# Moving two output transposes from steps 8 and 9 to steps 12 and 13, and one eviction from VectorE to ScalarE

## The chip, the cores and the metric

The kernel runs on one core of a Trainium2 chip. Its engines are TensorE (PE in the profile; PEld is its weight load), VectorE (DVE), ScalarE (ACT), GpSimd (POOL) and SyncE (SP), whose queue issues nearly all DMAs here. The metric is the device time of one execution in microseconds, as the median of several runs.

## The reference

Two blocks follow one another. All data are 32-bit floats in the reference's terms; the weights arrive as 64-bit floats and are converted in the kernel.

```python
# attention: x is [8, 8, 512, 64], state is [8, 8, 32, 64]
a = softmax(scale * x @ state.T)          # per batch and head, 512 x 32
xread = a @ state                         # 512 x 64
a2 = softmax(scale * state @ x.T)         # 32 x 512
sread = a2 @ x                            # 32 x 64
attn = concatenate([xread, sread], axis=2)
# bridge: heads side by side, 8 * 544 tokens of 512
h = tokens @ w_in                         # 512 -> 2048
g = h * cos(h)
out = g @ w_out                           # 2048 -> 512
```

## The kernel before, in words

**Steps.** A batch is worked off in 16 steps, one for each 128 of the 2048 hidden columns (`NF` = 16, `NH` = 8, a half). Eight batches of 512 tokens make 128 steps; 16 more steps treat the 256 state rows of all batches together. The order of the work on every engine is written out by hand: the loop at the end of the function goes through the steps and emits the instructions in the order in which each engine's queue shall run them. "Step 8 of batch 3" below is the pass of that loop with `t.b` = 3 and `s` = 8.

**One step.** `hidden` (L471) lets PE compute h for the step into one of two PSUM buffers (`hps`, tile `h`, two buffers). Its weights `sw` are `w_in` already multiplied with the state (`products`, L319, copied out at L445), its moving operand is the attention `aT`. Then the cosine factor: `gate` (L567) on ScalarE rounds h, `gate2` (L570) on VectorE subtracts, `gate3` (L573) on ScalarE takes the sine, `gate4` (L580) on VectorE multiplies by h into a slot of `g_all`. With `gate4` the h buffer comes free, and as there are two, `hidden` of step s needs `gate4` of step s-2. Three steps later `output` lets PE multiply g with blocks of `w_out` (`product`, L624, in two PSUM banks, MAIN and SIDE, of two halves each).

**Seven products for eight.** The products with `w_out` are made for pairs of batches (0 and 1, 2 and 3, and so on) by a scheme that needs seven block products where the plain one needs eight, with sums of g blocks before (`minus`, L586, on VectorE and GpSimd) and of results behind. A pair's four phases are the two halves of the hidden columns of its two batches. Results that are needed again are kept in three `held` tiles: `keep_product` takes a finished product out of PSUM, one half with ScalarE (L635), the other with VectorE (L637); `plus` (L630) adds a product to a held one; `total` (L644) adds held ones. The first and the fifth product of each pair go through `keep_product`: the fifth at the end of step 10 of the pair's odd batch. For phases 0 to 2 of batches 2 to 7 `hidden` is replaced by a similar scheme with seven half-size products (`hidden_a`, `hidden_b`, L514, with sums at L544 to L546 and L559, L560).

**Stores.** `store` does not emit anything at once. It appends two entries to the list `later`, one for each half; so does `total`. Each step takes at most one entry out of `later`, between `gate3` and `gate4`. A store's entry is a transpose of 32 x 32 blocks on VectorE (L651) from the held tile into one of two `ot` buffers and four DMAs on SP's queue (L657).

In batches 3, 5 and 7 the last product of the pair before ends in step 7 (`p4`, which then queues the two stores of that pair's even batch, second half of its columns). So steps 8 and 9 take one entry each, and `later` is empty from then on until step 2 of the next batch.

**Attention beside it.** While batch b is worked off, `plan` spreads the attention of batch b+1 over the same steps: for batches 3 and 5 the tokens' transposes (L301) in steps 1 and 2, scores and maxima in steps 5 and 6 (L333, spread by L339 in step 6), the shift (L356), row maxima (L349) and exps (L360, L365) in steps 6 and 7, sums in step 8 (L333, L375, L376), the norm in step 9 (L386), the state's part on PE in steps 10 to 12 (`turn` L392, copied by L397; `reads` L409; `keep` L419). Behind the reads of step 12 SP issues the loads of x for a later batch (L292, L115). In step 11 of an odd batch VectorE forms the differences (`halves`, L493) that the next batch needs. Batch 7 has no next batch, and none of this.

**Tail.** In the 16 steps of the state rows two blocks of `w_out` are read again (L197 on SP, emitted in the first of them) into the place of x, and converted from step 5 and step 7 of that part on (L228 and what follows).

Of the kernel before, what the change touches and what calls it, by code (L numbers as in the profile page):

```python
# [13 lines left out]
ACTF = mybir.ActivationFunctionType  # L14
# [3 lines left out]
TWO_PI = 2.0 * math.pi  # L18
# [3 lines left out]
def kernel(  # L22
# [8 lines left out]
    nc = tc.nc  # L31

    B, H, S, D = x.shape
# [9 lines left out]
    scale = 1.0 / math.sqrt(D)  # L43
# [23 lines left out]
    NH = NF // 2  # L67
# [58 lines left out]
    def load_state(half, queues):  # L126
        b = slice(4 * half, 4 * half + 4)
        for k in range(NK):
# [11 lines left out]
    acc = [[ops.tile([P, S], F32, name=f"o{m}{ch}") for ch in range(2)]  # L140
           for m in range(2)]
# [311 lines left out]
    def part(b, name, *args):  # L453

        if b not in attn:
            attn[b] = Attention(b)
        getattr(attn[b], name)(*args)
        if (name, args) == ("reads", (1,)) and b + 1 < B:
            if b > 0:
                attn[b + 1] = Attention(b + 1)  # L460
                attn[b + 1].load_tokens()
            load_x(b + 1)
# [125 lines left out]
    MAIN, SIDE = 0, 1  # L588
# [33 lines left out]
    def product(bank, w, g, i):  # L622
        for ch in range(2):
            nc.tensor.matmul(out=acc[bank][ch],  # L624
                             lhsT=w[:, i, P * ch:P * ch + P], rhs=g.g,
                             start=(i == 0), stop=(i == NH - 1))
        return i == NH - 1

    def plus(out, bank, ch, b):
        nc.vector.scalar_tensor_tensor(out=out.t[:, ch], in0=acc[bank][ch],  # L630
                                       scalar=TWO_PI, in1=b.t[:, ch],
                                       op0=ALU.mult, op1=ALU.add)

    def keep_product(out, bank):
        nc.scalar.activation(out.t[:, 0], acc[bank][0], func=ACTF.Copy,  # L635
                             scale=TWO_PI)
        nc.vector.tensor_scalar(out.t[:, 1], acc[bank][1], TWO_PI, None,  # L637
                                op0=ALU.mult)

    later = []  # L640

    def total(out, a, b):
        for ch in range(2):
            later.append(lambda ch=ch: nc.vector.tensor_tensor(  # L644
                out.t[:, ch], a.t[:, ch], b.t[:, ch], op=ALU.add))

    def store(b, half, src):

        def go(ch):
            ot = osb.tile([P, S], F32, name="ot")  # L650
            nc.vector.transpose(out=ot.rearrange("p (j i) -> p j i", i=32),  # L651
                                in_=src.t[:, ch].rearrange(
                                    "p (j i) -> p j i", i=32))
            rows = out[b * T:b * T + S, :].rearrange("(j t) d -> t j d", t=32)
            for q in range(P // 32):
                c0 = HD * half + P * ch + 32 * q
                nc.sync.dma_start(  # L657
                    out=rows[:, :, c0:c0 + 32],
                    in_=ot[32 * q:32 * q + 32].rearrange(
                        "p (j i) -> p j i", i=32))  # L660
            src.done()
        later.extend([lambda: go(0), lambda: go(1)])
# [16 lines left out]
    def free(t):  # L679
        g_free.append(t.slot)  # L680
# [18 lines left out]
    def output(t):  # L699
        if t.pair is None:  # L700
            state_output(t)
            return
        pr, i = t.pair, t.i
        if t.phase < 3 and pr.before and i % 3 < 2:
            pr.before.more(1)
        if t.phase == 0:
            if product(MAIN, a11, t, i):
                pr.u = Held()
                keep_product(pr.u, MAIN)
        if t.phase == 1:  # L710

            bank = MAIN if pr.before else SIDE
            if product(bank, a12, t, i):
                o = Held()
                for ch in range(2):
                    plus(o, bank, ch, pr.u)
                store(2 * pr.n, 0, o)
        if t.phase == 2:
            if product(MAIN, s1, pr.b[0, i], i):
                pr.p5 = Held()  # L720
                keep_product(pr.p5, MAIN)
        if t.phase == 3:
            last = product(SIDE, s4, t, i)
            free(t)
            if last:
                o = Held()
                for ch in range(2):
                    plus(o, SIDE, ch, pr.p5)
            product(MAIN, s2, pr.b[0, i], i)
            free(pr.b[0, i])  # L730
            if last:
                for ch in range(2):
                    plus(pr.u, MAIN, ch, pr.u)
                total(o, o, pr.u)
                store(2 * pr.n + 1, 0, o)
# [12 lines left out]
    def state_output(t):  # L748
        if t.n_th < NF - N_LAST:
            for i in range(2):  # L750
                state_product(t, i)
            t.last_pair.more(2)
            free(t)
            return
        kept_back.append(t)
        if len(kept_back) == N_LAST:
            t.last_pair.more(2 * N_LAST)
            for i in range(2):
                for u in kept_back:
                    state_product(u, i)  # L760
                state_store(i)
# [36 lines left out]
    def warm(n, to):  # L798

        for _ in range(n):  # L800
            nc.tensor.matmul(out=to, lhsT=zeros[:, 0:P], rhs=zeros, start=True,
                             stop=True)
# [124 lines left out]
    for step, t in enumerate(all_tiles):  # L927
        s = step % NF
        if s == 0 and t.b < B:
            steps = plan(t.b)  # L930
        todo = [p[s] if t.b < B else [] for p in steps]

        def go(n):
            for p in todo[n]:
                part(*p)

        last, conv = conv_at.get(step - 1, -1), conv_at.get(step, -1)
        if step == B * NF + (0 if f64 else 8):
            fetch(N_LOADS + 2)
        if step == 4:  # L940
            warm(1, acc[MAIN][0])
        ahead = all_tiles[step + 1:step + 3]
        if seven(t):
            if t.f % 2 == 0:
                hidden_b(t)
                sums_b(t)
                if s == NF - 2 and seven(all_tiles[step + 2]):
                    halves(t.b + 1)
        elif step != 1:
            hidden(t)  # L950
        first = len(ahead) > 1 and seven(ahead[0]) and ahead[0].f % 2 == 0
        if first:
            if not seven(t):

                h = t.hp
                take_slot(t)
                nc.scalar.copy(t.g, h)
            hidden_a(*ahead)
        if step == 0:
            hidden(all_tiles[1])  # L960
            warm(3, acc[MAIN][0])
            gate(t)
            gate2(t)
            convert(3, "bcdf")
            convert(4, "1")
            go(0)
        else:
            go(0)
            if step == 5:
                states(1, acc[SIDE][1])  # L970
            if not (seven(t) and t.f % 2):
                gate(t)
            gate2(t)
            if step == 3:
                warm(4, acc[MAIN][0])
                part(0, "products", 1, SIDE)
            if first:
                sums_a(ahead[0])
            go(1)
            go(3)  # L980
            if step == 1:
                convert(4, "bcdf")
            elif last >= 0:
                convert(last, "bcdf")
            if conv >= 0 and not todo[1]:
                convert(conv, "1")
        gate3(t)
        if seven(t) and t.f % 2 == 0:
            gate(t.second)
        if step == 3:  # L990
            part(0, "products_kept", 1, SIDE)
        if later:
            later.pop(0)()
        for u, new in zip(all_tiles[step + 2:step + 4], (False, True)):
            if seven(u) and u.f % 2 == 0 and new_pair(u) == new:
                sw_sums(u)
        gate4(t)
        if conv >= 0 and todo[1] and step > 0:
            convert(conv, "1")
        if t.pair is not None:  # L1000
            sums(t)
        if step == 6:
            states_kept(1, acc[SIDE][1])
        go(2)
        if conv >= 0:
            convert(conv, "2")
        go(4)
        for u in all_tiles[step + 5:step + 6]:
            if seven(u) and new_pair(u):
                halves(u.b)  # L1010
        if step in block_at:
            blocks(*block_at[step])
        if t.pair is not None:
            sums2(t)
        while len(line) >= (LAG if step >= 2 * NH else LAG + 1):
            output(line.pop(0))
        line.append(t)
# [32 lines left out]
```

## Time and profile before

| what | value |
|---|---|
| median of 8 runs | 766.31 us (765.78 to 767.26) |
| the profiled execution's own time | 766.22 us |
| its span, first to last instruction | 764.4 us |
| granted TensorE clock, mean | 0.997 |
| PE busy | 751.8 us, 98% |
| VectorE busy | 520.4 us, 68% |
| ScalarE busy | 316.0 us, 41% |
| GpSimd busy | 249.5 us, 33% |
| L651 on VectorE | 32 instructions, 22.2 us, mean 692 ns |
| L637 on VectorE | 8 instructions, 5.4 us, mean 680 ns |
| L635 on ScalarE | 8 instructions, 4.7 us, mean 592 ns |
| output stores on SP (L657) | 128 DMAs of 64 KB, landing after 2.0 us in the median |

All times within the profile are microseconds from the start of the span. Durations of instructions that follow one another overlap a little, as an instruction may start before the one ahead has been drained; what an instruction adds to its engine's queue is read from start to start. Ends of matmuls are modelled, so PE's busy share says less than the distances between its starts. The chain of waits is followed back from the last instruction: a line's entry there is time that the end of the program hung on.

### The profile page before, as it was taken

To read this page: it belongs to the slowest core of one execution; us is meant where nothing else is said; L and a number is where in the kernel's file an instruction comes from. 1 tells how busy PE (TensorE), PEld (TensorE's weight loads), DVE (VectorE), ACT (ScalarE), POOL (GpSimd) and SP (SyncE) were. 2 spreads that over 40 slices of the span, in tenths; PEclk is the share of its full clock that TensorE was granted. 3 is DMA by queue.
4 is the path that set the end of the run, shared out by engine and by line. 5 is a ranking of instruction groups with operands and counts; after the bars stand their busy time and mean duration, and the time that the engine had idled before them with its cause. 6 is when DMAs were issued, how large, how long until landed. Compare 5 with 4: busy or idle time off the path is not lost.

```text
span 764.4 us, 8416 instructions
## 1 busy us (share of the span) xinstructions
PE 751.8 (98%) x2880; PEld 380.8 (50%) x2880; DVE 520.4 (68%) x862; ACT 316.0 (41%) x523; POOL 249.5 (33%) x258
## 2 busy tenths in 40 slices
PE   8998999999999999999999999999999999999997
PEld 4443443445555554445555553445555554455554
DVE  4778787836896788847886789747878676432431
ACT  3877944533254335333362336333443333212212
POOL 2344278777121210662221111751211206500200
PEclk9999999999999999999999999999999999999999
DMA  8595471060002510340105210420100115000021
GB/s 247 165 276 175 146 119 29 4 107 1 14 15 48 90 28 3 54 83 0 28 2 94 44 28 15 68 56 1 27 1 1 28 28 138 0 0 15 14 42 41
DMA packets 161962, 43.54 MB, mean 57 GB/s; under 512 B 153920, under 2 KB 153920, under 8 KB 161920
## 3 DMA queue, kind: packets, MB, share of 16 engines
q1 hardware_dynamic: 161024, 42.49, 25.6%
q10 hardware_dynamic: 768, 0.39, 0.2%
q8 instruction: 23, 0.38, 0.2%
q0 software_dynamic: 128, 0.13, 0.1%
q14 instruction: 19, 0.16, 0.1%
HBM read 34.08 MB, written 8.91 MB: 56 GB/s over the span
## 4 chain that ended last, share of the span: by engine, by line
PE 88%; DVE 7%; ACT 2%; issue 1%; DMA 1%; POOL 1%; SPq 0%; DVEq 0%; ACTq 0%; POOLq 0%
PE o L624 47%; PE h L514 14%; PE h L471 14%; PE at L319 4%; PE o L744 4%; PE at L409 2%; PE o L319 1%; DVE xT L339 1%; DVE q L570 1%; DVE g_all L580 1%; DVE i L333 1%; ACT q L567 1%; PE at L392 1%; DVE aT L356 1%; DMA x_b<-in_x_dram 1%
## 5 line engine op out<-in xcount | busy, mean ns | idle before, releaser
L624 PE MATMUL o<-g_all,w_out 128*128 128x512 f32 x512 | 236.4, 598 | 0.3 <-POOL w_out L242 0.3
L624 PE MATMUL o<-g_all,s 128*128 128x512 f32 x384 | 177.3, 598 | 0.0
L586 POOL TENSOR_TENSOR g_all<-g_all 128x512 f32<-128x512 f32 x80 | 112.8, 1434 | 120.3 <-DVE g_all L580 120.3
L624 PEld LDWEIGHTS o<-g_all,w_out 128*128 128x128 f32 x512 | 93.8, 190 | 112.7 <-issue 108.0
L573 ACT ACTIVATE q<-q,halfpi 128x512 f32<-128x512 f32 (+1 forms) x144 | 100.8, 700 | 97.3 <-DVE q L570 97.2
L624 PEld LDWEIGHTS o<-g_all,s 128*128 128x128 f32 x384 | 70.8, 190 | 88.1 <-issue 82.1
L570 DVE TENSOR_TENSOR q<-q,h 128x512 f32<-128x512 int32 (+1 forms) x69 | 42.8, 621 | 102.5 <-ACT q L567 102.5
L471 PE MATMUL h<-aT,sw 128*128 128x512 f32 x224 | 106.1, 597 | 4.8 <-DVE g_all L580 4.3
L567 ACT ACTIVATE q<-g_all 128x512 int32<-128x512 f32 x75 | 46.8, 624 | 141.8 <-DVE g_all L560 141.4
L567 ACT ACTIVATE q<-h 128x512 int32<-128x512 f32 (+1 forms) x69 | 37.6, 545 | 128.5 <-PE h L471 128.5
L570 DVE TENSOR_TENSOR q<-q,g_all 128x512 f32<-128x512 int32 x75 | 52.6, 702 | 35.5 <-ACT q L567 35.5
L471 PEld LDWEIGHTS h<-aT,sw 128*128 128x128 f32 x224 | 41.5, 190 | 60.2 <-issue 44.2
L509 POOL TENSOR_TENSOR swS<-sw 128x128 f32<-128x128 f32 x35 | 17.4, 496 | 148.6 <-PE h L514 107.3
L580 DVE TENSOR_TENSOR g_all<-g_all,q 128x512 f32<-128x512 f32 x75 | 53.9, 719 | 14.5 <-ACT q L573 14.4
L580 DVE TENSOR_TENSOR g_all<-h,q 128x512 f32<-128x512 f32 (+1 forms) x69 | 42.8, 620 | 23.5 <-ACT q L573 23.1
L242 POOL TENSOR_TENSOR w_out<-w_out,s 128x1024 int32<-128x1024 int32 x10 | 23.9, 2393 | 77.5 <-DVE w_out L237 71.3
L509 POOL TENSOR_TENSOR swS<-sw,swS 128x128 f32<-128x128 f32 x35 | 18.3, 523 | 87.3 <-PE h L514 86.8
L514 PEld LDWEIGHTS h<-aT,sw 128*128 128x128 f32 x144 | 27.4, 190 | 34.4 <-issue 28.0
L514 PE MATMUL h<-aS,sw 128*128 128x256 f32 x144 | 43.1, 381 | 0.1
L514 PE MATMUL h<-aS,swS 128*128 128x256 f32 x144 | 42.8, 379 | 0.0
L514 PE MATMUL h<-aT,sw 128*128 128x256 f32 x144 | 42.8, 379 | 0.0
L586 DVE TENSOR_TENSOR g_all<-g_all 128x512 f32<-128x512 f32 x48 | 33.5, 697 | 1.6
(107 smaller groups left out, 888.4 us busy)
## 6 DMA issues: line engine op xcount, KB each, us to landing
out_dram<-ot SPq DMA_DIRECT2D x132, 64.0 KB, 2.0
g_all<-in_moe_w_out_dram SPq DMA_DIRECT2D x8, 1024.0 KB, 5.0
g_all<-in_moe_w_in_dram SPq DMA_DIRECT2D x6, 1024.0 KB, 5.4
xT<-in_x_dram SPq DMA_DIRECT2D x96, 64.0 KB, 2.5
x_b<-in_x_dram SPq DMA_DIRECT2D x24, 256.0 KB, 4.6
x_b<-in_x_dram SPq DMA_DIRECT2D x16, 128.0 KB, 4.1
g_all<-in_moe_w_in_dram SPq DMA_DIRECT2D x4, 512.0 KB, 6.0
x_b<-in_moe_w_out_dram SPq DMA_DIRECT2D x1, 1024.0 KB, 5.7
```

The costliest lines, as they stand in the source:

```text
L242: nc.gpsimd.tensor_tensor(bits, bits, e, op=ALU.add)
L319: nc.tensor.matmul(out=(to or at)[j][Ns * k:Ns * k + Ns, 0:n], lhsT=w[D * j:D * j + D, self.b, Ns * k:Ns * k + Ns], rhs=r(slice(D * j, D * ...
L471: nc.tensor.matmul(out=t.hp, lhsT=t.lhs(i), rhs=t.rhs(i), start=(i == 0), stop=(i == t.kn - 1))
L509: engine.tensor_tensor(o, x1, x2, op=op)
L514: nc.tensor.matmul(out=out, lhsT=w, rhs=r, start=True, stop=True)
L567: nc.scalar.activation(t.q.bitcast(I32), t.hp, func=ACTF.Copy, bias=0.25)
L570: nc.vector.tensor_tensor(t.q, t.q.bitcast(I32), t.hp, op=ALU.subtract)
L573: nc.scalar.activation(t.q, t.q, func=ACTF.Sin, bias=halfpi, scale=-TWO_PI)
L580: nc.vector.tensor_tensor(t.g, t.hp, t.q, op=ALU.mult)
L586: engine.tensor_tensor(out, a, b, op=ALU.subtract)
L624: nc.tensor.matmul(out=acc[bank][ch], lhsT=w[:, i, P * ch:P * ch + P], rhs=g.g, start=(i == 0), stop=(i == NH - 1))
L744: nc.tensor.matmul(out=acc[MAIN][i], lhsT=t.g[:, P * i:P * i + P], rhs=w_out[:, :, t.f, :], start=(t.n_th == 0), stop=(t.n_th == NF - 1))
```

## The change

```diff
-    def keep_product(out, bank):
-        nc.scalar.activation(out.t[:, 0], acc[bank][0], func=ACTF.Copy,
-                             scale=TWO_PI)
+    def keep_product(out, bank, scalar=False):
+
+        for ch in range(2 if scalar else 1):
+            nc.scalar.activation(out.t[:, ch], acc[bank][ch], func=ACTF.Copy,
+                                 scale=TWO_PI)
+        if scalar:
+            return
         nc.vector.tensor_scalar(out.t[:, 1], acc[bank][1], TWO_PI, None,
                                 op0=ALU.mult)
...
         if t.phase == 2:
             if product(MAIN, s1, pr.b[0, i], i):
                 pr.p5 = Held()
-                keep_product(pr.p5, MAIN)
+                keep_product(pr.p5, MAIN, pr.n > 0)
...
-        if later:
+
+
+        full = t.b % 2 == 1 and 1 < t.b < B and NH - 1 <= s < NH + 4
+        if later and not full:
             later.pop(0)()
```

`full` is true in steps 7 to 11 of batches 3, 5 and 7. In these steps nothing is taken out of `later`; the two entries that wait there, which before were taken in steps 8 and 9, are taken in steps 12 and 13. With each entry its transpose (L651) and its four DMAs (L657) are emitted there. The held tile that they read is given back in step 13 instead of step 9; the tiles that `Held` hands out are the same as before in every place.

The fifth product of the pairs 1 to 3 (step 10 of batches 3, 5 and 7) is taken out of PSUM by two ScalarE instructions instead of one on ScalarE and one on VectorE. That of pair 0 stays as it was. Nothing else is added, removed or moved.

## The prediction

> **What bounds the kernel now.** The first part of the page and a table by stretch come first: which engine is full, and is it full everywhere? The stretches are 38 or 39 us around steps 7 to 12 of batches 3, 5 and 7.
>
> ```profile
> PE 751.8 (98%) x2880; PEld 380.8 (50%) x2880; DVE 520.4 (68%) x862; ACT 316.0 (41%) x523; POOL 249.5 (33%) x258
> 286.00:324.00 38.00, 37.02 (x148) 16.80 (x133) 34.01 (x54) 16.24 (x27) 12.56 (x9) 1.00 0.16 26
> 453.00:492.00 39.00, 38.03 (x151) 17.22 (x150) 34.40 (x55) 16.54 (x27) 13.28 (x9) 1.00 0.16 26
> 618.00:656.00 38.00, 38.00 (x110) 17.76 (x109) 23.12 (x36) 12.95 (x21) 15.03 (x10) 1.00 0.30 76
> ```
>
> Columns of the last three: length, then busy time of PE, PEld, DVE, ACT and POOL, then PE's clock. PE is the bound with 98%. What can be won without taking matmuls away is its idle time. Batches 3 and 5 show 0.98 and 0.97 us of it, beside a VectorE busy for 34 us; batch 7, which prepares no attention of a next batch, shows none. So the change can pay in two of its three batches only.
>
> Second, the chain of waits across batch 3's stretch: who carries the time while PE stands?
>
> ```profile
> 303.64 0.04 DVE i L376
> ...
> 303.92 0.65 DVE ot L651
> 304.57 0.59 DVE g_all L580
> ...
> 307.53 1.80 DVE aT L386
> 309.33 0.62 DVE ot L651
> 309.95 0.59 DVE g_all L580
> 310.54 0.04 issue
> 310.58 1.98 PE h L471 x4
> ```
>
> From 290.12 (L560) to 310.58 the chain lies on VectorE and, for the exps, on ScalarE; then it goes back to PE and stays there. The two L651 pieces are the transposes that steps 8 and 9 make for the stores: the change moves exactly these. L580 is the gate's last product; it frees the h buffer that `hidden` needs two steps on.
>
> Third, PE's own timeline there.
>
> ```profile
> 303.05 1.98 PE L624 MATMUL o<-g_all,s 128*128 128x512 f32 x4
> 305.20 1.99 PE L471 MATMUL h<-aT,sw 128*128 128x512 f32 x4 [0.18 <-DVE g_all L580]
> 307.02 1.04 PE L392 MATMUL at<-ident,xT 128*128 128x128 f32 x8
> 307.90 1.88 PE L624 MATMUL o<-g_all,s 128*128 128x512 f32 x4
> 310.58 1.98 PE L471 MATMUL h<-aT,sw 128*128 128x512 f32 x4 [0.80 <-DVE g_all L580]
> ```
>
> Ends are modelled, so I count from start to start. Four matmuls in an unbroken run take 1.72 us (296.78 to 298.50), and 1.82 behind the small ones of L319 (636.40 to 638.22 in batch 7). `hidden(10)` could start at 303.05 + 1.82 = 304.87 and starts at 305.20: 0.33 lost, and 0.10 more for the restart (1.82 to the next, not 1.72). `hidden(11)` could start at 307.90 + 1.72 = 309.62 and starts at 310.58: 0.96 lost, and 0.10 for the restart. PE loses 1.49 us per batch here; that is the most that any relief of VectorE can give.
>
> **The two transposes leave steps 8 and 9.** From L651's start to L580's start behind it: 303.92 to 304.50 is 0.58, 309.25 to 309.88 is 0.63; batch 5 has 0.58 and 0.62 (471.21 to 471.79, 476.54 to 477.16). Does L580 move forward by all of it? It also needs ScalarE's sine: in step 8 that ended at 303.48 (302.76 + 0.72), before the 303.92 at which L580 would now start; in step 9 it started at 307.64 behind VectorE's own L570, and moves with it. So L580 comes 0.58 earlier in step 8 and 1.21 earlier in step 9.
>
> One thing could eat the first 0.58. L386, the norm of step 9, took 1.80 us here against a median of 1.23 over the eight of the kernel, and GpSimd's two subtractions of step 8 ran from 305.23 to 308.24, into it. L386 ended 1.09 us after them, so it looks as if it had stood behind GpSimd. But that pair starts on L580 of step 8 (24.63 us waited for it, start 0.08 after its end): it moves 0.58 earlier with it, so I count the gain whole; with GpSimd fixed in time it would be 0.63 per batch. [...]
>
> On PE: `hidden(10)`'s buffer comes free for a start at 305.20 - 0.58 = 304.62, before the 304.87 at which PE is ready, so that wait goes. PE is then ready for `hidden(11)` at 304.87 + 1.72 + 0.88 (L392) + 1.72 = 309.19, and the buffer lets it start at 310.58 - 1.21 = 309.37. A wait of 0.18 is left, still on VectorE, so the gain is the chain's 1.21, not PE's 1.49. Batch 5 gives 1.20 in the same way. Behind it PE has work without a wait (buffer of `hidden(12)`: L580 ends at 313.33, PE comes at 317.06), so the gain is kept to the end. Batch 7: 0, no PE idle to remove.
>
> **The fifth product goes to ScalarE alone** (step 10 of batches 3, 5 and 7). These rows are batch 3's, from the timelines of VectorE and ScalarE.
>
> ```profile
> 313.36 0.80 DVE L586 TENSOR_TENSOR g_all<-g_all 128x512 f32<-128x512 f32 x1
> 314.09 0.68 DVE L637 TENSOR_SCALAR held<-o 128x512 f32<-128x512 f32 x1
> 314.69 0.67 DVE L570 TENSOR_TENSOR q<-q,h 128x512 f32<-128x512 int32 x1
> ...
> 312.98 0.60 ACT L635 ACTIVATE held<-o 128x512 f32<-128x512 f32 x1
> 313.46 0.60 ACT L567 ACTIVATE q<-h 128x512 int32<-128x512 f32 x1
> ```
>
> VectorE loses 0.60 (314.09 to 314.69), ScalarE gains 0.48 (312.98 to 313.46). What stands behind the new eviction on ScalarE is L567 of step 11, and L570 waits for that: it would end at 313.46 + 0.48 + 0.60 = 314.54 instead of 314.06, where L570 now starts at 314.69. So L570 of step 11 comes at best 0.1 earlier. Nobody on PE waits there: `hidden(13)` starts at 323.43 and its buffer was free at 316.84, 6.6 us before. Its new wait on PE ends before it begins (that product's matmuls end at 309.78), and the bank's second half is written again only from some 315.3 on. In batch 7 L567 of step 11 waited 0.87 us for PE behind L635, which holds the 0.48. I take 0; without the 6.6 us of cover it would be a loss of up to 0.48 per batch, and it can't gain, since PE is not idle there.
>
> **What the transposes meet in steps 12 and 13.** In step 12 one lies ahead of L580 (322.79), 0.6 us; in step 13 it falls into the 1.49 us that L580 waited for ScalarE (328.21). `hidden(14)` starts at 329.79 with its buffer free at 323.48, `hidden(15)` at 334.94 with 328.90: 6.3 and 6.0 us of cover for 0.6. The two `ot` buffers were last used in steps 3 and 4 and their stores land within 3.1 us. Cost 0.
>
> **The DMAs on SP's queue.** Each transpose takes four stores along. In batches 3 and 5 they go behind the twenty loads of x that step 12 issues (L292 from 313.66, L115 to 331.51), which can then not be held up by them; the stores' data is nobody's input. In batch 7 two reloads of weights (L197, issued at 639.56 and 640.13) now stand behind stores that leave only after step 13's transpose, near 655.9, with some 2 us of issue: about 18 us later. They land within 7.8 us, near 667, and ScalarE first reads them at 698.91: over 30 us of cover. Cost 0.
>
> **Sum.** 1.21 + 1.20 = 2.41 us from the profiled execution's 766.22 (span 764.4 and 1.8 around it) gives 763.81; the median of the runs, 766.31, lies 0.09 above that execution, so 763.9.
>
> **Rivals.** (a) *Half*: GpSimd's subtractions do not move with L580, and L386 still ends where it did; only the step 9 transposes count: 766.3 - 1.25 = 765.1. For it: the 1.80; against: the 0.08 us between L580's end and GpSimd's start. (b) *Nothing*: another wait of PE takes the place, most likely on ScalarE's L573 of steps 8 and 9: 766.3. Against: that sine was ready 0.44 us before the new start. (c) *All of PE's idle time*: shorter instructions on VectorE without the 0.18 left: 766.3 - 2 x 1.49 = 763.3. (d) *Slower*: batch 7's two reloads, put behind the moved stores, come late for L228 at 698.91, and with them the products that need that weight; PE stands for as long. It decides only when they land more than 30 us later than I work out, that is 50 us later than now. 4 us beyond that, about one step's PE work in batch 7, would leave 766.3 - 2.4 + 4 = 767.9. The queue order speaks for it, the margin against it. The edit itself does what it says: in each of the three batches exactly two transposes wait in steps 8 to 11, and steps 12 and 13 have nothing else to take.
>
> **Chances.** Forecast 0.79, (a) 0.08, (b) 0.06, (c) 0.03, (d) 0.04. A measurement of this kernel tells about 0.2%, 1.5 us, from no change. The forecast and (c) are beyond that: faster 0.82. (a) and (b) lie within: 0.14. Slower: 0.04. The range goes from (c), 763.2, to (a), 765.1; (b), (d) and a little of the edges are left out.
>
> **What would show it.** In the changed profile: no L651 between L376 and L580 in step 8, nor behind L386 in step 9; `hidden(10)` without its wait, `hidden(11)` with about 0.2 left; GpSimd's step 8 pair still 0.1 behind L580 and L386 still near 1.8; PE idle in the two stretches about 0.6 to 0.8 less in the table's modelled busy time; L635 eleven times, L637 five; L197 near 657; batch 7 without PE idle. L386 longer by 0.6 means (a); a PE wait on ScalarE in steps 8 to 11 means (b); a PE stop near 700 means (d).

## The result, and the profile after

The changed kernel takes 763.36 us in the median (762.58 to 764.44, 10 runs), the kernel before 766.06 (28 runs of the same session). The ratio is 0.9965, interval 0.9957 to 0.9973: 2.7 us less, from 2.1 to 3.3. The profiled execution of the changed kernel took 763.10 us with a span of 761.3.

Behind the fifth product's eviction the changed kernel's lines are shifted: the transpose for the store is L655 (was L651), the eviction on ScalarE L637 (was L635) and that on VectorE L641 (was L637). Everything up to the eviction has the lines that it had.

First the page's sum of busy time and the table by stretch, as before: length, then PE, PEld, VectorE, ScalarE, GpSimd, and PE's clock. The first two stretches hold steps 7 to 12 of batches 3 and 5, the third those of batch 7.

```profile
PE 750.1 (99%) x2880; PEld 380.2 (50%) x2880; DVE 519.2 (68%) x859; ACT 317.4 (42%) x526; POOL 249.7 (33%) x258
286.00:324.00 38.00, 37.96 (x150) 17.04 (x149) 32.42 (x52) 17.31 (x28) 14.17 (x10) 1.00 0.12 20
450.00:492.00 42.00, 41.80 (x175) 18.70 (x174) 35.18 (x56) 19.78 (x33) 15.48 (x11) 1.00 0.15 25
615.00:656.00 41.00, 41.00 (x117) 19.03 (x116) 23.78 (x37) 13.54 (x23) 17.34 (x12) 1.00 0.12 19
```

PE's modelled idle time in them is 0.04, 0.20 and 0 us, where it was 0.98, 0.97 and 0. VectorE has three instructions fewer (859 for 862) and ScalarE three more (526 for 523): the three evictions.

The chain of waits across batch 3's steps 8 to 11, in the changed kernel:

```profile
302.06 1.92 PE o L624 x4
303.97 1.72 PE h L471 x4
305.69 0.87 PE at L392 x8
306.56 1.72 PE o L624 x4
308.28 0.04 issue
308.33 1.98 PE h L471 x4
310.31 1.02 PE at L409 x16
```

Before, this place read DVE at L376, L651, L580, L386, L651, L580. Now the chain stays on PE.

PE's timeline of the changed kernel in the same place:

```profile
301.99 1.99 PE L624 MATMUL o<-g_all,s 128*128 128x512 f32 x4
303.81 1.88 PE L471 MATMUL h<-aT,sw 128*128 128x512 f32 x4
305.53 1.04 PE L392 MATMUL at<-ident,xT 128*128 128x128 f32 x8
306.40 1.88 PE L624 MATMUL o<-g_all,s 128*128 128x512 f32 x4
308.33 1.98 PE L471 MATMUL h<-aT,sw 128*128 128x512 f32 x4
310.24 1.09 PE L409 MATMUL at<-x_b,xT 128*64 128x128 f32 x16
```

`hidden(10)` (303.81) starts 1.82 us behind the products, PE's own pace there: no wait. `hidden(11)` was ready at 306.40 + 1.72 = 308.12 and starts at 308.33: 0.21 late, where the prediction left 0.18.

From here on I use one measure for all kernels: the time on PE from the start of `hidden(8)` to the start of the reads (L409) of the same batch. It holds all that VectorE could cost PE in steps 8 to 11, and no start-up. Before it is 15.71 us in both batches (296.78 to 312.49, 464.07 to 479.78). Without PE's losses, put at 1.49 before, it would be 14.22. In the changed kernel it is 14.51 in batch 3 (295.73 to 310.24) and 14.78 in batch 5 (461.82 to 476.60): a gain of 1.20 and of 0.93, together 2.13.

The two profiled spans differ by more, by 3.1 us. Of that, 1.05 lies ahead of batch 3's `hidden(8)` (295.73 against 296.78), before the first instruction that the change touches. The granted clock between 5 and 15 us was 1.00 in this execution and 0.83 in that of the kernel before: there the trace has it at 0.50 from 8.29 to 11.71 us, and by the matmul at 12.4 us 0.8 of the 1.05 has arisen. What is left, 2.1, is the local gain.

### The profile page after: what moved, and what is told of

It is laid out like the page before. It is cut to its first block, busy times and chain, and to the rows that moved or that the text cites. A ratio compares the mean times of both kernels' runs of the same rounds, so it can differ in the third digit from the quotient of the medians.

```text
span 761.3 us, 8424 instructions
## 1 busy us (share of the span) xinstructions
PE 750.1 (99%) x2880; PEld 380.2 (50%) x2880; DVE 519.2 (68%) x859; ACT 317.4 (42%) x526; POOL 249.7 (33%) x258
## 4 chain that ended last, share of the span: by engine, by line
PE 90%; DVE 5%; ACT 2%; DMA 1%; POOL 1%; issue 1%; SPq 0%; ACTq 0%; DVEq 0%; POOLq 0%
PE o L624 49%; PE h L514 14%; PE h L471 14%; PE at L319 4%; PE o L748 4%; PE at L409 2%; PE o L319 1%; PE at L392 1%; DVE xT L339 1%; DVE q L570 1%; DMA x_b<-in_x_dram 1%; DVE i L333 1%; DVE g_all L580 0%; ACT q L567 0%; DVE aT L356 0%
## 5 line engine op out<-in xcount | busy, mean ns | idle before, releaser
L570 DVE TENSOR_TENSOR q<-q,h 128x512 f32<-128x512 int32 (+1 forms) x69 | 42.9, 621 | 102.4 <-ACT q L567 102.3
L567 ACT ACTIVATE q<-g_all 128x512 int32<-128x512 f32 x75 | 46.8, 624 | 142.2 <-DVE g_all L560 141.8
L567 ACT ACTIVATE q<-h 128x512 int32<-128x512 f32 (+1 forms) x69 | 37.6, 545 | 128.4 <-PE h L471 128.4
L570 DVE TENSOR_TENSOR q<-q,g_all 128x512 f32<-128x512 int32 x75 | 52.7, 702 | 36.0 <-ACT q L567 36.0
L580 DVE TENSOR_TENSOR g_all<-g_all,q 128x512 f32<-128x512 f32 x75 | 53.9, 719 | 14.4 <-ACT q L573 14.3
L580 DVE TENSOR_TENSOR g_all<-h,q 128x512 f32<-128x512 f32 (+1 forms) x69 | 42.8, 620 | 22.3 <-ACT q L573 21.4
```

What stands on the lines that cost most here:

```text
L567: nc.scalar.activation(t.q.bitcast(I32), t.hp, func=ACTF.Copy, bias=0.25)
L570: nc.vector.tensor_tensor(t.q, t.q.bitcast(I32), t.hp, op=ALU.subtract)
L580: nc.vector.tensor_tensor(t.g, t.hp, t.q, op=ALU.mult)
```

## The experiments

Each kernel's short diff is against the changed kernel. "Hold" stands for the empty steps 7 to 11, "eviction" for the fifth product on ScalarE alone. The last two columns are the measure just given; a smaller number is a gain.

| run | median us | kernel before | ratio, interval | batch 3 | batch 5 |
|---|---|---|---|---|---|
| kernel before | | 766.06 | 1 | 15.71 | 15.71 |
| changed kernel | 763.36 | 766.06 | 0.9965 [0.9957, 0.9973] | 14.51 | 14.78 |
| e1_hold_only | 763.68 | 766.15 | 0.9966 [0.9955, 0.9977] | 14.50 | 14.51 |
| e2_evict_and_batch7 | 766.73 | 766.15 | 1.0007 [0.9995, 1.0018] | 15.70 | 15.98 |
| e3_one_step_later | 765.53 | 766.15 | 0.9994 [0.9984, 1.0003] | 15.09 | 15.39 |
| e4_gpsimd_pair_later | 763.47 | 766.15 | 0.9965 [0.9951, 0.9979] | 14.21 | 14.32 |
| e5_evict_pairs_2_3 | 764.22 | 766.11 | 0.9971 [0.9959, 0.9983] | 14.51 | 14.51 |
| e6_one_more_on_scalare | 763.51 | 766.11 | 0.9964 [0.9950, 0.9977] | 14.51 | 14.52 |
| e7_two_more_on_scalare | 763.08 | 766.11 | 0.9960 [0.9946, 0.9973] | 14.51 | 14.51 |
| e8_hold_and_gpsimd_later | 762.73 | 766.11 | 0.9958 [0.9946, 0.9971] | 14.20 | 14.20 |
| e9_six_more_in_step_12 | 764.24 | 766.06 | 0.9978 [0.9965, 0.9991] | 14.52 | 14.51 |
| e10_fourteen_more_in_step_12 | 778.83 | 766.06 | 1.0171 [1.0153, 1.0190] | 14.52 | 14.51 |
| e11_three_more_on_scalare | 764.78 | 766.37 | 0.9983 [0.9972, 0.9994] | 14.51 | 14.80 |
| e12_changed_and_one_more | 763.04 | 766.37 | 0.9960 [0.9942, 0.9977] | 14.52 | 14.51 |

The intervals reach 0.6 to 1.4 us to either side, so run times alone can't place a few tenths; the traces do that. Each kernel has one trace.

**Which of the parts brings it: the hold in batches 3 and 5 alone, or the eviction and batch 7?**

```diff
 e1_hold_only
-                keep_product(pr.p5, MAIN, pr.n > 0)
+                keep_product(pr.p5, MAIN)
 e2_evict_and_batch7
-        full = t.b % 2 == 1 and 1 < t.b < B and NH - 1 <= s < NH + 4
+        full = t.b == 7 and NH - 1 <= s < NH + 4
```

> The changed kernel, but with the fifth product evicted by both engines as before; only the transposes are held. My theory (the whole gain is VectorE's queue in steps 8 and 9): 2.4 us faster than before, the same as the changed kernel within 0.3; from the start of hidden(8) to the start of the reads in batch 3 PE takes 14.5 us as in the changed kernel (15.7 before). Rival (the eviction gives part of it, since VectorE loses 0.6 us in step 10): about 0.3 us per batch less gain, 1.5 to 1.8 us faster than before.

> The two parts that I costed at nothing, together and alone: the fifth product on ScalarE in pairs 1 to 3, and the transposes held in batch 7 only. My theory: the time of before within 0.5 us; in batch 3 hidden(8) to the reads still 15.7 us; the two late weight reloads issued near 657 and PE without a stop near 700. Rival (the 0.3 us that the result shows beyond my sum come from here): 0.3 to 0.9 us faster. Rival (late reloads): slower, with PE idle near 700.

The hold alone has the whole gain (0.9966 against 0.9965), and eviction with batch 7's hold have none: the interval of e2 takes in 1. In e2 the two reloads of weights (L197) are issued at 660.54 and 661.11, 21 us later than before (18.4 when the 2.6 us are taken off by which its batch 7 comes later), and PE is busy throughout 615 to 730: the moved DMAs cost nothing. Something unexpected stands in the last column: with the eviction, batch 5 is 0.27 us slower (14.78 against 14.51, and 15.98 against 15.71).

In step 11 itself, the place that the prediction looked at, the moved eviction makes VectorE's L570 wait for ScalarE. From ScalarE's and VectorE's timelines of the changed kernel, batch 3:

```profile
310.72 1.09 ACT L637 ACTIVATE held<-o 128x512 f32<-128x512 f32 x2
311.69 0.61 ACT L567 ACTIVATE q<-h 128x512 int32<-128x512 f32 x1
```

```profile
312.33 0.69 DVE L570 TENSOR_TENSOR q<-q,h 128x512 f32<-128x512 int32 x1 [0.41 <-ACT q L567]
```

PE has no stop there: `hidden(12)` to `hidden(13)` takes 6.37 us as before (314.80 to 321.17, and 317.06 to 323.43).

**Does each of the two transposes count by itself?** In e3 only step 8 is kept empty, so that the transposes are in steps 9 and 10.

```diff
-        full = t.b % 2 == 1 and 1 < t.b < B and NH - 1 <= s < NH + 4
+        full = t.b % 2 == 1 and 1 < t.b < B and s == NH
```

> The changed kernel with the hold in step 8 alone, so that the two transposes of batches 3, 5 and 7 fall into steps 9 and 10. My theory: L580 comes 0.58 us earlier in both step 8 and step 9, since one transpose still lies behind L386; hidden(8) to the reads 15.1 us in batches 3 and 5, and 1.2 us faster than before in all, half of the change. Rival (GpSimd's pair of step 8 pins L386, so what is saved in step 8 is lost): 15.7 us, no gain. Rival (what counts is only to empty step 8): the whole 2.4 us.

Batch 3 gives 15.09, half of the gain, as expected. Batch 5 gives 15.39, short of that by the loss just named, so the 1.2 us expected in all shrink to 0.94 in the trace. The time, 0.9994, can't be told from no change. VectorE's timeline of e3 has step 9's transpose between the norm and L580, as before:

```profile
306.94 1.79 DVE L386 TENSOR_TENSOR aT<-aT,xT 128x1024 f32<-128x1024 f32 x1
308.65 0.70 DVE L655 STREAM_TRANSPOSE ot<-held 128x512 f32<-128x512 f32 x1
309.28 0.65 DVE L580 TENSOR_TENSOR g_all<-h,q 128x512 f32<-128x512 f32 x1
```

**What keeps the norm at 1.8 us?** The prediction took it that L386 stands behind GpSimd's two subtractions of step 8. In e4 these are emitted behind the two of step 9, in batches 3 and 5 alone.

```diff
         if t.phase == 3:
             minus(pr, pr.b[0, i].g, t.g, pr.b[0, i].g, True)
-            minus(pr, pr.b[2, i].g, t.g, pr.b[2, i].g)
+            if not (t.b in (3, 5) and i == 0):
+                minus(pr, pr.b[2, i].g, t.g, pr.b[2, i].g)
...
         if t.phase == 3:
+            if t.b in (3, 5) and i == 0:
+                return
             minus(pr, pr.b[1, i].g, pr.b[1, i].g, pr.b[0, i].g)
+            if t.b in (3, 5) and i == 1:
+                minus(pr, pr.b[2, 0].g, pr.b[3, 0].g, pr.b[2, 0].g)
+                minus(pr, pr.b[1, 0].g, pr.b[1, 0].g, pr.b[0, 0].g)
```

> The changed kernel, and in batches 3 and 5 GpSimd's two subtractions of step 8 put behind those of step 9 in its queue, so that GpSimd stands still while VectorE runs L386. If GpSimd stretches L386: L386 takes 1.23 us instead of 1.80, L580 of step 9 comes 0.57 earlier, the last wait of hidden(11) goes (0.2 and 0.1 for the restart), hidden(8) to the reads 14.2 us, and the kernel is 0.4 to 0.6 us faster than the changed one. If L386's 1.80 us has another cause: L386 stays at 1.80, no gain. Loss if GpSimd's longer backlog reaches the differences of step 11 and PE behind them: up to 3 us per batch, but there are 6 us of cover.

Here is VectorE in the changed kernel, with GpSimd's pair from its timeline behind it:

```profile
302.87 0.63 DVE L580 TENSOR_TENSOR g_all<-h,q 128x512 f32<-128x512 f32 x1
...
305.87 1.80 DVE L386 TENSOR_TENSOR aT<-aT,xT 128x1024 f32<-128x1024 f32 x1
307.59 0.68 DVE L580 TENSOR_TENSOR g_all<-h,q 128x512 f32<-128x512 f32 x1
```

```profile
303.57 3.01 POOL L586 TENSOR_TENSOR g_all<-g_all 128x512 f32<-128x512 f32 x2 [24.03 <-DVE g_all L580]
```

And VectorE in e4, then GpSimd there:

```profile
306.45 0.65 DVE L570 TENSOR_TENSOR q<-q,h 128x512 f32<-128x512 int32 x1
307.02 1.21 DVE L386 TENSOR_TENSOR aT<-aT,xT 128x1024 f32<-128x1024 f32 x1
308.15 0.68 DVE L580 TENSOR_TENSOR g_all<-h,q 128x512 f32<-128x512 f32 x1
```

```profile
308.91 4.70 POOL L586 TENSOR_TENSOR g_all<-g_all 128x512 f32<-128x512 f32 x3 [28.21 <-DVE g_all L580]
```

In the changed kernel GpSimd's pair starts 0.07 behind the end of L580 (303.50) and ends at 306.58; L386 ends 1.09 us after it, the same 1.09 as before. With the pair out of the way L386 takes 1.21 instead of 1.80, and `hidden(11)` has no wait left: 14.21 in batch 3, the floor of 14.22. So it was GpSimd's pair that held L386 up; by what means is not shown. The gain, 0.30 us in batch 3 and 0.46 in batch 5, is plain in the trace; the 0.4 to 0.6 us expected in all can't be seen in the run times (0.9965 for both).

**The best version.** e8 joins the hold, the eviction as it was, and GpSimd's pair of e4.

> The transposes held, no eviction moved, and GpSimd's pair of step 8 of batches 3 and 5 behind that of step 9: what the runs so far point to as the best. Theory: hidden(8) to the reads 14.21 us in both batches, PE without a wait there; 2.98 us less than before and 0.9 us less than the changed kernel, so about 763.1 where before has 766.1. Rival (the pause comes back at another place): 14.3 or more in one of the batches.

Both batches reach 14.20, so the losses of 1.49 us per batch are gone. The 762.73 is the lowest median of the study, but its interval overlaps that of the changed kernel: that it is the faster of the two is shown by the traces alone.

**Where does the eviction lose 0.27 us in batch 5?** The chain of waits around L567 of step 6 of batch 5 is the first place in which the kernels with and without the loss differ. First the kernel before, then the changed one:

```profile
458.14 0.04 issue
458.19 0.64 ACT q L567
```

```profile
455.89 0.32 issue
456.21 0.64 ACT q L567
```

ScalarE stands 0.28 us longer before the same instruction, with nothing that it waits for. Counted in the trace from the start of ScalarE's stream, waits on semaphores that are instructions of their own included, it is the 448th instruction in the changed kernel, in e2, e3 and e4, which all have a loss, and the 447th in the kernel before and in e1, which have none. The other theory was that the eviction itself, or its place in time, delays that batch. e5 leaves the eviction out of batch 3, e6 and e7 put one or two repeated evictions on ScalarE in batch 3 where the hold stands alone; e11 puts three, and e12 adds one to the changed kernel, so that L567 is at another place again.

```diff
 e5_evict_pairs_2_3
-                keep_product(pr.p5, MAIN, pr.n > 0)
+                keep_product(pr.p5, MAIN, pr.n > 1)
 e6, e7, e11 (1, 2 and 3 times)
-                keep_product(pr.p5, MAIN, pr.n > 0)
+                keep_product(pr.p5, MAIN)
+                for _ in range(1 if pr.n == 1 else 0):
+                    nc.scalar.activation(pr.p5.t[:, 0], acc[MAIN][0],
+                                         func=ACTF.Copy, scale=TWO_PI)
 e12
                 keep_product(pr.p5, MAIN, pr.n > 0)
+                for _ in range(1 if pr.n == 1 else 0):
+                    nc.scalar.activation(pr.p5.t[:, 0], acc[MAIN][0],
+                                         func=ACTF.Copy, scale=TWO_PI)
```

> The changed kernel, with the fifth product on ScalarE alone only in pairs 2 and 3, so that ScalarE's stream up to step 6 of batch 5 holds no added instruction. In the changed kernel and the three others with the eviction of batch 3 moved, ScalarE's 448th instruction is L567 of that step and started some 0.3 us after it was ready; in the two without it the 448th is another one. Theory (a pause bound to the place in ScalarE's stream, pushed onto the path by one added instruction): hidden(8) to the reads 14.5 us in batch 5 as in batch 3, against 14.78 in the changed kernel. Rival (chance of one execution): 14.5 or 14.8 at random. Rival (the eviction of batch 5 itself costs it): 14.8.

> Only the transposes held, no eviction moved, but ScalarE evicts the fifth product's first half twice in batch 3: one instruction more in its stream, and nothing taken from VectorE. Theory (place in the stream): L567 of step 6 of batch 5 is again the 448th, starts 0.3 us late, and hidden(8) to the reads in batch 5 is 14.8 us. Rival (VectorE's missing eviction or chance): 14.5 us.

> The same with two instructions more. Theory: the pause falls on the instruction ahead of that L567, before which ScalarE stands idle for some 4 us, and is hidden: 14.5 us in batch 5, less than with one instruction more. Rival (every added ScalarE instruction costs): 14.8 us or more.

> Only the transposes held, ScalarE's eviction of the fifth product's first half in batch 3 made four times. With one more instruction that L567 was ScalarE's 446th, with two more its 447th (the waits that stand as instructions of their own shift it too), so here it should be the 448th. Theory (place in the stream): it starts 0.3 us late again, and hidden(8) to the reads in batch 5 is 14.8 us, though VectorE keeps its half of the eviction. Rival (the moved eviction itself, or chance): 14.5 us.

> The changed kernel, with ScalarE evicting the first half of batch 3's fifth product once more. Theory (place): L567 of step 6 of batch 5 is no longer the 448th, and hidden(8) to the reads in batch 5 is 14.5 us with one ScalarE instruction more than the changed kernel has. Rival (the moved eviction itself costs it): 14.8 us or more.

e5 has no loss. e6 was to bring L567 to the 448th place and didn't: it became the 446th, because other waits became instructions of their own or ceased to be, and batch 5 takes 14.52 instead of the 14.8 expected. So e6 says nothing for the place, but it speaks against "every added instruction on ScalarE costs". e7 has it at the 447th, and no loss; its 14.5 came as expected, but not by the way expected, since L567 did not pass the 448th place. e11 has it at the 448th, and the loss is there without any moved eviction; the chain of e11, then ScalarE's timeline in the changed kernel and in e12:

```profile
456.87 0.34 issue
457.21 0.64 ACT q L567
```

```profile
456.21 0.63 ACT L567 ACTIVATE q<-g_all 128x512 int32<-128x512 f32 x1 [5.16 <-DVE g_all L560]
```

```profile
458.67 0.63 ACT L567 ACTIVATE q<-g_all 128x512 int32<-128x512 f32 x1 [4.88 <-DVE g_all L560]
```

e12 has the eviction, L567 at the 447th place, the idle time of the kernels without a loss (4.88 us; the changed kernel has 5.16), and batch 5 is 14.51. Over all fourteen kernels L567 is the 448th in five, and these lose in batch 5 against batch 3: 0.27 to 0.30 us in the changed kernel, e2, e3 and e11, and 0.11 in e4, where the norm of batch 5 takes 1.21 us and `hidden(11)` starts without a wait (473.46 to 475.18). It is at an earlier place in nine, and there the two batches agree within 0.01. That the loss goes with the place and not with the eviction is shown. What the pause is stays open. In the five kernels a transfer of 8 KB on the queue q14, of the kind that the profile calls "instruction", starts 0.64 to 0.92 us behind this L567; but in the kernel before, which has no pause there, one starts 0.96 us behind it (459.15). That the two belong together is not shown.

**How much cover do steps 12 and 13 have?** e9 and e10 repeat the moved transpose of step 12, in batches 3 and 5, seven and fifteen times in all; the eviction is as it was.

```diff
+            for _ in range(1 + extra[0]):
-            nc.vector.transpose(out=ot.rearrange("p (j i) -> p j i", i=32),
-                                in_=src.t[:, ch].rearrange(
-                                    "p (j i) -> p j i", i=32))
+                nc.vector.transpose(
+                    out=ot.rearrange("p (j i) -> p j i", i=32),
+                    in_=src.t[:, ch].rearrange("p (j i) -> p j i", i=32))
...
+            extra[0] = 6 if t.b in (3, 5) and s == NH + 4 else 0
```

> Only the transposes held, and the transpose of step 12 in batches 3 and 5 made seven times instead of once: 3.7 us more on VectorE ahead of L580. My theory (5.7 us of cover there in the changed kernel): no cost; hidden(13) to hidden(15) 11.5 us in batch 3 as in the changed kernel. Rival (moved work costs its length wherever it stands): up to 3.7 us per batch.

> The same with fifteen transposes: 8.7 us more. My theory: 8.7 less the cover of 5.7 leaves 3.0 us, and 0.1 for the restart, per batch: hidden(13) to hidden(15) 14.6 us in batches 3 and 5, and 6 us slower than with the hold alone. Rival (more slack further on, in the second h buffer): less than 1 us. Rival (no cover): 17 us slower.

From `hidden(13)` to `hidden(15)` on PE e9 takes 11.52 us (320.67 to 332.19), as the changed kernel does (321.17 to 332.69): six more cost PE nothing. Its median of 764.24 is no cost either: its three runs with a mean granted clock of 1.000 took 762.74 to 763.13, the five of the changed kernel 762.58 to 763.61. e10 takes 19.30 where 14.6 was expected. Its VectorE timeline (the transpose is L657 there), then its PE timeline, in batch 3:

```profile
321.52 11.16 DVE L657 STREAM_TRANSPOSE ot<-held 128x512 f32<-128x512 f32 x15
332.71 0.69 DVE L580 TENSOR_TENSOR g_all<-h,q 128x512 f32<-128x512 f32 x1
```

```profile
322.15 1.88 PE L471 MATMUL h<-aT,sw 128*128 128x512 f32 x4
323.96 1.09 PE L319 MATMUL at<-w_in,st_all 64*32 64x512 f32 x16
324.98 3.70 PE L624 MATMUL o<-g_all,s 128*128 128x512 f32 x8
333.46 3.78 PE L471 MATMUL h<-aT,sw 128*128 128x512 f32 x4 [4.78 <-DVE g_all L580]
337.03 4.58 PE L624 MATMUL o<-g_all,s 128*128 128x512 f32 x8
341.45 1.88 PE L471 MATMUL h<-aT,sw 128*128 128x512 f32 x4
```

Fourteen more are 14 x 0.74 = 10.4 us here (one transpose after another into the same tile takes 0.74, not 0.62). The cover is 5.6 to 5.7: in the changed kernel `hidden(14)`'s buffer is free at 321.87, where L580 ends, and PE comes at 327.54. That makes PE about 4.8 late, and it is: PE would start `hidden(14)` at 322.15 + 6.37 = 328.52 (321.17 to 327.54 is 6.37) and starts at 333.46, 4.9 late. But the loss is 19.30 - 11.52 = 7.78 per batch. The table by stretch of e10 has the rest (the clock is the first number behind the last x):

```profile
328.00:333.00 5.00, 0.68 (x2) 0.00 (x0) 4.76 (x8) 0.00 (x0) 0.00 (x0) 0.92 1.14 207
333.00:337.00 4.00, 3.54 (x4) 1.51 (x5) 3.69 (x6) 0.72 (x1) 3.52 (x3) 0.50 0.56 89
337.00:342.00 5.00, 5.00 (x11) 2.26 (x10) 3.02 (x4) 1.32 (x2) 4.84 (x7) 0.80 0.22 35
342.00:350.00 8.00, 8.00 (x27) 4.42 (x25) 3.85 (x7) 2.49 (x5) 4.04 (x4) 1.00 0.01 2
```

After the stop the granted clock is 0.50. The rows' means give its length: 0.92 over 5 us is 0.8 us at 0.50, and 0.80 over 5 us is 2.0 us, so it was 0.50 from some 332.2 to 339.0 us, or 6.8 us. The four matmuls of `hidden(14)` take 3.57 to the next start instead of 1.72, the next eight 4.42 instead of 3.43: 2.84 more. With the 4.94 of the stop that is the loss of 7.78. So the expected 3.0 per batch missed in both terms: fourteen more transposes cost 10.4 us and not 8.7, and the restart cost 2.84 and not 0.1. The clock fell some 3.5 us behind the modelled end of the last matmul (328.68) and was back 5.5 us after the restart. The stops of 0.2 to 1 us in batches 3 and 5 of the kernels before and after show no fall (1.00 in their stretches of the tables).

## Why the prediction was right, and where it was off

It said 763.9 us, from 763.2 to 765.1, faster; 763.36 was measured. The mechanism is the one forecast. That the median lies within the range, 0.16 above its lower end, owes something to chance, as the sum below shows. Its steps, one by one:

- **The two transposes, 1.21 us per batch: right in size and place.** Batch 3 gained 1.20. The 0.58 and the 0.63 count separately, as e3 shows with 15.09. The reason was right too: GpSimd's pair moved with L580, so the first 0.58 was not eaten, and rivals (a), half the gain, and (b), nothing, fall.
- **The wait of 0.18 left before `hidden(11)`: right**, 0.21 measured. PE's modelled idle time fell by 0.94 and 0.77 us where 0.6 to 0.8 was forecast. e4 shows that the wait that is left is the norm held up by GpSimd. Rival (c), all of PE's idle time gone, is what e8 is.
- **The eviction at 0: mis-sized, -0.27 us in batch 5.** The bound of 0.48 was for work queued behind the eviction in step 11, and that was rightly judged to be hidden: L570 of step 11 now waits 0.41 us for ScalarE, and PE has no stop there. What the step left out is that L567 of step 6 of batch 5 moves from the 447th to the 448th place in ScalarE's stream, and an unexplained pause, 0.32 us there, then falls on an instruction that VectorE's chain hangs on. So the second 1.20 of the sum was 0.93.
- **Steps 12 and 13 at 0: right.** Of the 6.3 us of cover in step 12 the transpose took 0.6, and 5.7 are left. What it costs when the cover is gone the prediction doesn't say; in e10 a stop of 4.9 us cost 7.8.
- **DMAs on SP's queue at 0: right.** L197 was issued at 654.76 and 655.34, 15.2 us later by the profile's clock; with the 3.2 us by which batch 7 comes earlier that is 18.4, as predicted. L228 read the first at 695.73, more than 30 us after the landing. Rival (d) falls.
- **Batch 7 at 0: right**, PE without idle time before and after; e2 shows the rest.
- **The sum.** It was 2.41; the trace shows 1.20 + 0.93 = 2.13, and the runs 2.7 with 2.1 to 3.3. The median is 0.54 below the forecast: 0.25 of it because the kernel before took 766.06 and not 766.31, the rest because 2.7 is more than 2.41. Runs with a granted clock of 1.000 in their mean have 765.03 us before (median of 8, from the experiments' sessions) and 762.75 changed (of 5), which is 2.3. So the rest of the 2.7 lies, as far as can be argued, in stretches of half clock early in the program, which some executions have and others don't (last section); no run here isolates them.

## What to carry to other kernels

Find the stretch in which the bounding engine idles, follow the chain back to the engine that it hangs on, and look there for work whose result nobody waits for: move it to a place where the buffer of the next product is free for microseconds before it is used. Price it by the start-to-start distances and test the releaser of each neighbour: what starts on the moved instruction can move with it, as GpSimd's pair did with L580 (0.08 us behind its end before, 0.07 after). Where a change is worth a few tenths, measure it in the trace from one fixed instruction to another, since run times scatter by more than that (764.77 to 767.55 us for the kernel before).

## What the runs showed of the hardware that was not expected

- **A pause by place in ScalarE's stream.** In all five kernels in which ScalarE's 448th instruction is L567 of step 6 of batch 5, it starts 0.32 to 0.34 us behind the end of the wait ahead of it; at the 446th and 447th place it starts 0.045 behind. The 576th, 128 further on, shows 0.32 to 0.34 in the ten kernels in which it follows such a wait. In e6 the 448th follows another instruction directly and shows no pause. The cause is open.
- **A stop of 4.9 us cost 7.8.** The granted clock was 0.50 from some 332.2 to 339.0 us, until 5.5 us after the restart at 333.46 (e10).
- **The clock early in the program differs between executions of kernels that are the same up to there:** 0.83 and 0.83 in the stretches 5 to 10 and 10 to 15 us in the profile before, 1.00 and 1.00 in the changed one, 0.85 and 0.81 in e1. In the profile before and in e1 it is one stretch of 3.41 us at 0.50. e1 and five other profiles have one more near 75 us, and batch 3's `hidden(8)` starts 2.6 us later in e1 than before.
